# Sliding-window attention into a SwiGLU block: the opening's V loads moved behind a cast, and 11 dummy matmuls of 512 columns in place of 48 of 121

## The chip, the cores and the metric

The kernel runs on one core of one Trainium2 chip. The metric is the device time of one execution in microseconds (us). The three timed executions of the kernel before took 328.53, 329.00 and 329.53 us, a median of 329.0.

The core has five engines with a queue of instructions each: TensorE (PE; the profile lists its weight loads apart, as PEld), VectorE (DVE), ScalarE (ACT), GpSimd (POOL) and SyncE (SP). Transfers between main memory and the on-chip memory run on 16 DMA engines. Those that GpSimd issues run in one software queue, q0 in the profile.

## The reference

```python
# attention: 8 batches, 8 heads, 576 tokens, 64 per head; window of 64 tokens, causal
scores = np.matmul(q, k.transpose(0, 1, 3, 2)) / np.sqrt(64)
rel = pos[:, None] - pos[None, :]
scores = np.where((rel >= 0) & (rel < 64), scores, -1e9)
attn = softmax(scores)
attn_out = np.matmul(attn, v)                       # 8 x 8 x 576 x 64
# the block behind it, on 4608 tokens of 512
x = attn_out.transpose(0, 2, 1, 3).reshape(4608, 512)
g = x @ w_gate                                      # 512 -> 1536
out = (g * sigmoid(g) * (x @ w_val)) @ w_out        # 1536 -> 512
```

## The kernel before

The 4608 tokens are cut into 36 tiles of 128 tokens for the attention and into 9 chunks of 512 tokens (four tiles) for the block behind it. All matmuls are in bf16.

For a tile, `S` computes the scores of all heads into two PSUM banks (lines 468 and 472), ScalarE takes the exponential into `pt` (line 480), `AVs` multiplies by V, which carries a column of ones for the sum (line 592), and `AVn` divides on VectorE: a reciprocal (line 608) and a product (line 611) into `xb`. `X` transposes `xb` on TensorE (line 723), and a copy puts it into `xT`. For a chunk, `F` multiplies `xT` by columns of Wg and of Wv (line 787), ScalarE and VectorE form the gated product `hT`, and `O` multiplies it by Wo (line 818) and stores the result.

The first four tiles have an order of their own, written out by hand in `build`. A score needs keys from the tile and from the half tile before it, so the V rows that stand across a tile's border are copied into shifted tiles `vs`: `shift(n, r, engine)` copies half `r` of V tile `n` (line 295, called from line 579). Tile 1 reads `vs` that `shift(0, 1)` and `shift(1, 0)` fill, tile 2 that of `shift(1, 1)` and `shift(2, 0)`, tile 3 that of `shift(2, 1)` and `shift(3, 0)`.

The opening in `build` runs as follows. `loads` issues the first keys from SP and ACT (line 734), and then, on GpSimd, the first queries, the second keys and the second queries (line 375), the making of the identity and of the masks (lines 317 and 326), the loads of V tiles 0 to 3 (line 366), those of the first columns of Wg and Wv (line 381), and four shifts. VectorE finishes the masks meanwhile (lines 330 to 335). `warm` has TensorE run 48 matmuls of 121 columns on zeros (line 762). `first_T` casts the first keys to bf16 on VectorE (line 295, tile `ost`) and transposes them on TensorE (line 746); `T2` does the like with queries and keys of 256 tokens (line 415). `Sbias` puts the mask into a PSUM bank by a matmul (line 448). Then come the scores of tiles 0 and 1, further transposes, `AVs` of tile 0, the scores of tile 2, `AVs` of tile 1, the scores of tile 3, `X` of tiles 0 and 1, one dummy matmul, `AVs` of tiles 2 and 3, and `F` on the first 256 tokens.

After the opening, a list of steps in the text `EARLY` and a regular loop set the order on the engines, and the lists `LOADS` and `SHIPS` set the order of GpSimd's loads and of SP's transposing transfers. Every operation of an engine runs in the order in which it was added; a small planner works out the semaphore waits from what each operation reads and writes. `self.hold`, given to a load as `after`, makes it wait for a named operation as well.

Of the kernel before, what the change touches and what calls it, by code (L numbers as in the profile page):

```python
# [166 lines left out]
class _Kernel:  # L167
# [234 lines left out]
    def T2(self, st, x, engs):  # L402
        g = self.g
        src = (self.ks2 if x == "k" else self.qs2)[st % 2]
        dst = self.kT if x == "k" else self.qT
        z0 = (2 * st) % self.NZ
        for cc in range(2):
            bank, bk = self.bank("a")
            tb = bank[:, 0:256].bitcast(BF).rearrange("p (c j t) -> p c j t", c=2, j=2)

            def pe(e, cc=cc, tb=tb):
                for c in range(2):
                    for j in range(2):
                        for p in range(2):
                            r = e.transpose(tb[64 * p:64 * p + 64, c, j, :], src[:, 4 * cc + 2 * c + p, j, :], self.ident[:, :])  # L415
                return r

            g.op("pe", pe, reads=["ident", ("s2", x, st % 2, 0), ("s2", x, st % 2, 1)], writes=[bk])
            d = dst[:, 2 * cc:2 * cc + 2, 128 * z0:128 * z0 + 256].rearrange("p c (t j) -> p c t j", j=2)
            a = tb.rearrange("p c j t -> p c t j")  # L420
            self.copy(engs[cc], d, a, [bk], [(x + "T", z, cc) for z in (z0, z0 + 1)])
            self.drop([(bank, bk)])
# [282 lines left out]
    def X(self, n, eng="sp", kind="f", half=False):  # L705
        if n >= NCH:
            return
        g = self.g
        ix, it, u = n % 4, (n // 4) % self.NX, n % 4
        xb = self.xb[ix]  # L710
        xo = self.xT[it][:, :, 128 * u:128 * u + 128]
        xk = [("xb", ix, 0), ("xb", ix, 1)]
        if eng == "sp":
            g.op("sp", lambda e: e.dma_start_transpose(xo, xb[:, :]), reads=xk, writes=[("xT", it, u)], dma=True)
            return
        bank, bk = self.bank(kind)
        tb = bank[:, 0:256].bitcast(BF).rearrange("p (c t) -> p c t", c=4)

        def pe(e):
            for c in range(4):  # L720
                for p in range(2 if half else 1):
                    w = 64 if half else 128
                    r = e.transpose(tb[w * p:w * p + w, c, :], xb[:, 128 * c + w * p:128 * c + w * p + w], self.ident[:, :])  # L723
            return r

        g.op("pe", pe, reads=["ident"] + xk, writes=[bk])
        self.copy(eng, xo, tb, [bk], [("xT", it, u)])
        self.drop([(bank, bk)])
# [38 lines left out]
    def F(self, c, fs, lo=0, hi=512):  # L767
        g = self.g
        nf, n = len(fs), hi - lo
        w = nf * n  # L770
        xT = self.xT[c % self.NX]
        xk = [("xT", c % self.NX, u) for u in range(lo // 128, hi // 128)]
        ih = c % self.NH
        i = self.n_s % self.NS
        self.n_s += 1
        sig, uu = self.sig[i], self.uu[i]
        out = self.hT[ih][:, fs[0]:fs[0] + nf, lo:hi]
        v3 = lambda a: a[:, 0:w].rearrange("p (f t) -> p f t", f=nf)
        bs = []
        for W, wk in ((self.Wg, "Wg"), (self.Wv, "Wv")):  # L780
            bank, bk = self.bank("f")
            bs.append((bank, bk))

            def pe(e, W=W, bank=bank):
                for a, f in enumerate(fs):
                    for kk in range(NK):
                        r = e.matmul(bank[:, a * n:a * n + n], W[:, kk, f * 128:f * 128 + 128], xT[:, kk, lo:hi],  # L787
                                     start=(kk == 0), stop=(kk == NK - 1))
                return r

            g.op("pe", pe, reads=xk + [(wk, f) for f in fs], writes=[bk], cost=w * 0.0017)
            if wk == "Wg":
                g.op("act", lambda e, G=bank: e.activation(sig[:, 0:w], G[:, 0:w], ACTF.Tanh, scale=0.5), reads=[bk], writes=[("sig", i)])  # L793
        (G, gk), (V, vk) = bs
        g.op("dve", lambda e: e.scalar_tensor_tensor(uu[:, 0:w], sig[:, 0:w], 1.0, G[:, 0:w], ALU.add, ALU.mult),  # L795
             reads=[("sig", i), gk], writes=[("uu", i)])
        g.op("dve", lambda e: e.scalar_tensor_tensor(out, v3(uu), 0.5, v3(V), ALU.mult, ALU.mult),  # L797
             reads=[("uu", i), vk], writes=[("hT", ih, f) for f in fs])
        self.drop(bs)
# [61 lines left out]
    def loads(self):  # L861
        self.first_loads()
        self.load2(0, "q")
        self.load2(1, "k")
        self.load2(1, "q")
        self.init()
        self.init_ident()
        self.init_mask()
        self.init_nmask()
        for n in range(4):  # L870
            self.load(n, "v")
        self.W(0, 2)
        self.load_w("g", 2, 4)
        self.shift(0, 1, "pool")
        self.shift(1, 1, "pool")
        self.load_w("v", 2, 4)
        self.shift(2, 1, "pool")
        self.shift(3, 0, "pool")
        self.W(4, 6)
        self.W(6, 8)  # L880

# [178 lines left out]
    def build(self):  # L1060
        F, S, AV, X, T2, O = self.F, self.S, self.AV, self.X, self.T2, self.O
        self.loads()
        self.banks("a", [4, 5, 6, 7, 0, 1, 2, 3, 4, 5, 0, 1, 2, 3, 4, 5, 6, 7, 0, 1, 2, 3, 4, 5, 6, 7, 6, 7])
        self.warm(48, n=121)
        self.first_T(("dve", "act"))
        s0 = self.Sa(0)
        T2(0, "q", ("act", "dve"))
        self.Sbias(s0)
        self.warm(2)
        self.Sb(s0)  # L1070
        s1 = self.Sa(1, True)
        self.Sb(s1)
        T2(1, "k", ("dve", "act"))
        T2(1, "q", ("dve", "act"))
        self.start()
        s2, s3 = self.Sa(2), self.Sa(3)
        a0, a1, a2, a3 = self.AVa(0), self.AVa(1), self.AVa(2), self.AVa(3)
        self.AVs(a0)
        self.shift(1, 0, "dve")
        self.AVn(a0)  # L1080
        self.shift(2, 0, "dve")
        self.Sbias(s2)
        self.Sb(s2)
        self.AVs(a1)
        self.AVn(a1)
        self.Sbias(s3)
        self.Sb(s3)
        X(0, "dve", "a")
        X(1, "dve", "a")
        self.warm(1, j=2)  # L1090
        self.AVs(a2)
        self.AVn(a2)
        self.AVs(a3)
        self.AVn(a3)
        F(0, (0, 1), 0, 256)
        X(2, "act", "a")
        X(3, "act", "a")
        F(0, (2, 3), 0, 256)
        F(0, (0, 1), 256, 512)
        for n in range(4):  # L1100
            self.did |= {w % n for w in ("s%d", "a%d", "x%d", "Tk%d", "Tq%d")}
        self.main("F0.2-3b")
        self.free = set(range(8))
        self.g.now = dict.fromkeys(self.g.now, max(self.g.now.values()))
        for t in self.program():
            self.pump()
            first = len(self.g.ops)
            self.main(t)
            self.at[t] = next((o for o in self.g.ops[first:] if o.eng == "pe"), None)
        self.pump()  # L1110
        assert not any(self.queues)
        self.g.emit()
# [42 lines left out]
```

## Time and profile before

| what | value |
|---|---|
| median of three executions | 329.0 us |
| the profiled execution, its own time | 329.18 us |
| its span | 327.4 us |
| TensorE busy | 316.7 us, 97% of the span |
| VectorE, ScalarE, GpSimd busy | 203.3, 137.0, 107.6 us |
| granted TensorE clock | 1.00 |
| read from and written to main memory | 37.75 and 9.44 MB |

The profile is of one execution. Its span is 1.8 us shorter than the time of the same execution; what lies around the span isn't in the trace. Durations below are from this execution. In a timeline, the columns are the start and the duration in us, the engine, the line of the kernel, the operation with its output and inputs, the number of instructions merged, and in brackets how long the engine was idle before and what ended that; "issue" there is time in which the engine waited for nothing that the profile shows. In the table by stages, the number in brackets behind an engine's busy time is the count of its instructions.

### The profile page before, as it was taken

The page shows a single profiled execution, that of the slowest core. Times are in us where ns is not written, and L with a number is a line of the kernel's source. Part 1 is how long each engine was busy: PE and PEld are TensorE (multiplying, and loading weights), DVE is VectorE, ACT ScalarE, POOL GpSimd, SP SyncE. Part 2 cuts the span into 40 slices and gives each one's busy share as a digit, 9 for nine tenths or more (in the row PEclk, how much of TensorE's full clock was granted, in tenths as well). Part 3 has the DMA queues.
Part 4 walks back from the last instruction along what each step waited for, and adds up shares of the span by engine and source line. Part 5 has one row for each costly group of instructions (what it writes and reads, how often), then busy time and mean ns, then how long its engine had stood idle before and what let it go on. Part 6 is the DMA issues. An engine that isn't in the chain of part 4 may idle for free.

```text
span 327.4 us, 8016 instructions
## 1 busy us (share of the span) xinstructions
PE 316.7 (97%) x3413; PEld 168.1 (51%) x3451; DVE 203.3 (62%) x352; ACT 137.0 (42%) x246; POOL 107.6 (33%) x138
## 2 busy tenths in 40 slices
PE   7899999999999999999999999999999999999997
PEld 6584576666455445444545454545454544444443
DVE  4677975676567935775757666665656566555520
ACT  2645865555234445242525252525252432332222
POOL 8899969645300000507060607060602000000000
DMA  9999999999999762949899999999997211100012
GB/s 139 178 186 183 187 195 157 160 181 161 148 156 160 127 147 66 101 107 120 127 130 113 135 139 108 137 122 132 120 138 87 55 45 49 49 32 33 34 58 103
DMA packets 157348, 39.33 MB, mean 120 GB/s; under 512 B 144384, under 2 KB 152832, under 8 KB 157312
## 3 DMA queue, kind: packets, MB, share of 16 engines
q0 software_dynamic: 109008, 18.62, 73.8%
q1 hardware_dynamic: 42848, 10.69, 22.8%
q10 hardware_dynamic: 5456, 9.51, 9.3%
q8 instruction: 27, 0.44, 0.6%
q14 instruction: 9, 0.07, 0.1%
HBM read 37.75 MB, written 9.44 MB: 144 GB/s over the span
## 4 chain that ended last, share of the span: by engine, by line
PE 93%; issue 2%; ACT 2%; POOL 1%; DVE 1%; POOLq 0%
PE ps L787 56%; PE ps L818 28%; PE ps L641 3%; PE ps L505 1%; PE ps L468 1%; PE ps L415 1%; PE ps L723 1%; PE ps L843 1%; ACT pt L480 1%; PE ps L472 1%; PE ps L592 1%; POOL qs L375 1%; ACT kT L293 0%; ACT qT L293 0%; PE ps L509 0%
## 5 line engine op out<-in xcount | busy, mean ns | idle before, releaser
L787 PE MATMUL ps<-xT,Wv 128*128 128x512 bf16 (+1 forms) x470 | 110.6, 357 | 1.1 <-issue 0.6
L787 PE MATMUL ps<-xT,Wg 128*128 128x512 bf16 (+1 forms) x461 | 107.1, 357 | 2.7 <-issue 2.5
L795 DVE SCALAR_TENSOR_TENSOR uu<-sig,ps 128x512 bf16<-128x512 bf16 x108 | 73.8, 683 | 57.2 <-ACT sig L793 57.2
L793 ACT ACTIVATE sig<-ps 128x512 bf16<-128x512 f32 x108 | 65.1, 603 | 74.1 <-PE ps L787 74.0
L818 PE MATMUL ps<-Wo,hT 128*128 128x512 bf16 x413 | 95.2, 379 | 0.5 <-issue 0.2
L797 DVE SCALAR_TENSOR_TENSOR hT<-uu,ps 128x512 bf16<-128x512 bf16 x108 | 74.1, 686 | 3.7
L787 PEld LDWEIGHTS ps<-xT,Wv 128*128 128x128 bf16 x480 | 47.0, 98 | 46.4
L787 PEld LDWEIGHTS ps<-xT,Wg 128*128 128x128 bf16 x480 | 45.0, 98 | 43.1 <-issue 0.8
L818 PEld LDWEIGHTS ps<-Wo,hT 128*128 128x128 bf16 x420 | 40.9, 98 | 49.1
L366 POOL DMA_DIRECT2D kn<-in_k_dram x29 | 25.2, 874 | 114.7 <-PE ps L818 69.0
L825 ACT ACTIVATE ost<-ps 128x512 f32<-128x512 f32 x35 | 20.9, 597 | 92.2 <-PE ps L818 92.2
L366 POOL DMA_DIRECT2D va<-in_v_dram x40 | 35.0, 893 | 17.1 <-PE ps L818 10.9
L366 POOL DMA_DIRECT2D qn<-in_q_dram x29 | 25.3, 874 | 8.3 <-DMA Wo<-in_moe_w_out_dram 2.9
L668 DVE RECIPROCAL rp<-ps 128x14 f32<-128x14 f32 (+1 forms) x28 | 5.7, 202 | 33.5 <-PE ps L641 33.5
L480 ACT ACTIVATE pt<-ps 128x512 bf16<-128x512 f32 x36 | 18.9, 599 | 6.6 <-PE ps L472 5.7
L517 ACT ACTIVATE pt<-ps 128x512 bf16<-128x512 f32 x36 | 18.6, 603 | 3.7 <-PE ps L509 3.7
L670 DVE TENSOR_TENSOR xb<-ps,rp 128x896 bf16<-128x896 f32 (+1 forms) x28 | 19.4, 692 | 1.0
L641 PEld LDWEIGHTS ps<-va,pt 64*64 64x64 bf16 x888 | 10.8, 107 | 6.1 <-issue 5.5
L641 PE MATMUL ps<-va,pt 64*64 64x65 bf16 x888 | 13.4, 194 | 0.1
L526 DVE TENSOR_TENSOR pt<-pt,kmask 128x1024 bf16<-128x1024 bf16 x18 | 12.3, 683 | 0.0
L526 DVE TENSOR_TENSOR pt<-pt,mask 128x1024 bf16<-128x1024 bf16 x14 | 9.6, 686 | 2.0 <-ACT pt L480 2.0
L472 PE MATMUL ps<-qT,kT 64*64 64x64 bf16 x288 | 7.6, 194 | 1.0 <-issue 1.0
(65 smaller groups left out, 145.1 us busy)
## 6 DMA issues: line engine op xcount, KB each, us to landing
out_dram<-ost ACTq DMA_DIRECT2D x35, 256.0 KB, 3.1
va<-in_v_dram POOLq DMA_DIRECT2D x32, 128.0 KB, 6.1
kn<-in_k_dram POOLq DMA_DIRECT2D x23, 128.0 KB, 5.4
qn<-in_q_dram POOLq DMA_DIRECT2D x23, 128.0 KB, 5.5
Wg<-in_moe_w_gate_dram POOLq DMA_DIRECT2D x6, 256.0 KB, 7.3
Wv<-in_moe_w_val_dram POOLq DMA_DIRECT2D x6, 256.0 KB, 7.3
Wo<-in_moe_w_out_dram POOLq DMA_DIRECT2D x2, 768.0 KB, 15.4
qs<-in_q_dram POOLq DMA_DIRECT2D x3, 256.0 KB, 6.8
```

The costliest lines, as they stand in the source:

```text
L366: self.g.op("pool", lambda e, d=d, a=a: e.dma_start(d, a), writes=ks, dma=True, after=self.hold)
L480: g.op("act", lambda e, po=po, p=p: e.activation(po, sv[p], ACTF.Exp, scale=SCALE), reads=[bx[p][1]], writes=[pk[p]])
L517: g.op("act", lambda e, po=po, p=p: e.activation(po, sv[p], ACTF.Exp, scale=SCALE), reads=[bx[p][1]], writes=[pk[p]])
L526: self.g.op("dve", lambda e: e.tensor_tensor(pt, pt, m, ALU.mult), reads=pk + [key], writes=pk)
L641: z = e.matmul(self.psa[64 * c:64 * c + 64, o:o + 65], pt[p][rows, h, 64 * a:64 * a + 64], va[m][rows, h, 0:65], start=first, stop=phase = ...
L670: g.op("dve", lambda e, d=d, num=num, rb=rb: e.tensor_tensor(d, num, rb, ALU.mult), reads=bk + [("rp", k)], writes=xk, cost=(1.0, 0.25)[k])
L787: r = e.matmul(bank[:, a * n:a * n + n], W[:, kk, f * 128:f * 128 + 128], xT[:, kk, lo:hi], start=(kk == 0), stop=(kk == NK - 1))
L793: g.op("act", lambda e, G=bank: e.activation(sig[:, 0:w], G[:, 0:w], ACTF.Tanh, scale=0.5), reads=[bk], writes=[("sig", i)])
L795: g.op("dve", lambda e: e.scalar_tensor_tensor(uu[:, 0:w], sig[:, 0:w], 1.0, G[:, 0:w], ALU.add, ALU.mult), reads=[("sig", i), gk], writes ...
L797: g.op("dve", lambda e: e.scalar_tensor_tensor(out, v3(uu), 0.5, v3(V), ALU.mult, ALU.mult), reads=[("uu", i), vk], writes=[("hT", ih, f) ...
L818: r = e.matmul(OB[:, :], hT[:, f, 128 * u:128 * u + 128], self.Wo[:, f, :], start=(f == 0), stop=(f == NF - 1), skip_group_check=mid is no ...
L825: g.op("act", lambda e: e.activation(ost[:, :], OB[:, :], ACTF.Copy), reads=[ok], writes=[("ost", io)])
```

## The change

Three things are changed, all in the opening.

The loads of V tiles 0 to 3, and all that follows them on GpSimd in the opening, move from `loads` into a new function `next_loads`, which is called after `first_T`. On GpSimd they still stand behind the masks; but the first V load now waits for VectorE's cast of the first keys (the first VectorE operation that `first_T` adds), and since GpSimd works in order, all behind it do.

The dummy matmuls at the start are 11 of 512 columns, where they were 48 of 121.

`shift(0, 1)` is done by VectorE, ahead of `shift(1, 0)`, and no longer by GpSimd. On GpSimd `shift(1, 1)` now stands ahead of the second load of Wg, and the second load of Wv behind `shift(3, 0)`.

```diff
         self.init_ident()
         self.init_mask()
         self.init_nmask()
+
+    def next_loads(self, after):
+        self.hold = after
         for n in range(4):
             self.load(n, "v")
+            self.hold = None
         self.W(0, 2)
+        self.shift(1, 1, "pool")
         self.load_w("g", 2, 4)
-        self.shift(0, 1, "pool")
-        self.shift(1, 1, "pool")
-        self.load_w("v", 2, 4)
         self.shift(2, 1, "pool")
         self.shift(3, 0, "pool")
+        self.load_w("v", 2, 4)
         self.W(4, 6)
         self.W(6, 8)
 
@@ build @@
-        self.warm(48, n=121)
+        self.warm(11)
+        first = len(self.g.ops)
         self.first_T(("dve", "act"))
+        self.next_loads(next(o for o in self.g.ops[first:] if o.eng == "dve"))
         s0 = self.Sa(0)
         T2(0, "q", ("act", "dve"))
         self.Sbias(s0)
...
         a0, a1, a2, a3 = self.AVa(0), self.AVa(1), self.AVa(2), self.AVa(3)
         self.AVs(a0)
+        self.shift(0, 1, "dve")
         self.shift(1, 0, "dve")
         self.AVn(a0)
         self.shift(2, 0, "dve")
```

## The prediction

> **What bounds the kernel now.** First the page: TensorE is busy for 97% of the span and carries 93% of the chain that ended last. So what counts is when its dense stream starts, and where it stops. Second, its own waits: beyond the first 7 us there are two holes worth the name, 1.0 us at line 472 and 0.6 us at line 787, both ended by "issue", which is no other engine.
>
> ```profile
> span 327.4 us, 8016 instructions
> PE 93%; issue 2%; ACT 2%; POOL 1%; DVE 1%; POOLq 0%
> q8 instruction: 27, 0.44, 0.6%
> PE ps L787 <- issue: 3.1, 17, 0.6
> PE ps L472 <- issue: 1.0, 1, 1.0
> ```
>
> Third, the chain in the opening and the timeline around 83 us, which place the holes: 14.18 to 15.21 us, inside the scores of tile 3, and 0.55 us before 83.58, inside one product of four matmuls. Nothing in the program separates the matmuls there.
>
> ```profile
> 14.03 0.15 PE ps L468
> 14.18 1.03 issue
> 15.21 0.22 PE ps L472 x2
> ...
> 83.58 0.38 PE L787 MATMUL ps<-xT,Wv 128*128 128x512 bf16 x1 [0.55 <-issue]
> ```
>
> Fourth, TensorE's instruction counts by stage.
>
> ```profile
> 0.00:9.28 9.28, 6.94 (x92) 5.98 (x97) 4.63 (x18) 2.57 (x4) 7.86 (x15) 1.00 1.12 143
> 9.28:14.50 5.22, 4.55 (x145) 2.82 (x135) 3.60 (x8) 4.13 (x8) 4.60 (x7) 1.00 2.06 172
> 14.50:16.30 1.80, 0.96 (x29) 0.80 (x29) 0.73 (x2) 0.64 (x2) 1.38 (x3) 1.00 1.45 196
> 16.30:83.50 67.20, 65.59 (x970) 43.34 (x980) 48.06 (x87) 38.40 (x71) 50.52 (x64) 1.00 1.72 174
> ```
>
> Between the holes lie 29 + 980 = 1009 weight loads, each with a matmul: 2018 instructions, and some 30 separate waits make 2048, or 8 x 256. The instruction queue q8 moved 27 packets, 0.44 MB: 16 KB each, or 256 instructions of 64 bytes, and 27 x 256 = 6912 is about TensorE's whole program (2 x 3451). I read the holes as TensorE at the end of its loaded code. The code packets next to them began at 12.82 and 81.30 us and took 0.95 us; TensorE went on 1.44 and 1.34 us after their ends. The DMA engines were at their fullest when the first was asked for.
>
> Fifth, the opening by engine: POOL and DVE rows, one launch of V each time, then the copies.
>
> ```profile
> 5.38 0.91 POOL L366 DMA_DIRECT2D va<-in_v_dram  x1
> 5.38 2.04 POOL L366 DMA_DIRECT2D va<-in_v_dram  x2
> 5.33 0.22 DVE L330 TENSOR_SCALAR mask<-mask 128x192 bf16<-128x192 bf16 x1 [2.62 <-POOL mask L326]
> 5.86 0.49 DVE L335 TENSOR_SCALAR nmask<-mask 128x384 bf16<-128x384 bf16 x1
> 6.27 0.67 DVE L295 CAST ost<-hT 128x1024 bf16<-128x1024 f32 x1
> 12.04 0.72 DVE L295 COPY vs<-va 64x512 bf16<-64x512 bf16 x1
> 14.92 0.61 POOL L295 COPY vs<-va 64x512 bf16<-64x512 bf16 x1 [1.00 <-DMA va<-in_v_dram]
> 20.25 1.04 PE L787 MATMUL ps<-xT,Wv 128*128 128x256 bf16 x8
> ```
>
> The launches of V overlap the mask's last step and the cast, and the second lasted 1.13 us where the others last about 0.9.
>
> **The change part by part.**
>
> *Dummies.* 48 of 121 columns ran from 1.29 to 6.01 us: 101 ns apart up to 5.5 us, 53 ns after (the rate had doubled). 11 of 512 at the same rates: 427 ns each, ten by 5.6 us, the last soon after. Both end about 1 us before the transposes at 7.00: 0 us. But 37 matmuls and 37 loads fewer move every edge of the code 74 instructions later in the program. The first hole stood behind load 222; it now stands behind load 259 of the old count, in the middle of AVs of tile 2 (the opening has 251 loads by 16.30). The edge before it, where the next block is asked for, moves from load 97 (9.28 us) to load 134 (10.52 us, in the second keys' transposes). From 9.28 to the release took 5.93 us; so the block is there at about 10.52 + 5.93 = 16.45 us. This hole isn't removed; it meets the other chain, next.
>
> *Copy moved to VectorE.* One more copy, 0.65 us from start to start as at 12.04, lies on VectorE ahead of both divisions. In order: copies from 12.04 and 12.69, reciprocal 13.34, product 13.56, copy 14.16, reciprocal 14.65, product from 14.88 to 15.57 (before: to 14.92). X of tile 1 follows at 15.62; before, the hole held it until 15.74. From there 0.58 us to AVs of tile 2 and 0.86 us more to the first F, as in the trace: F at 17.06, against 17.18. With the block arriving at 16.45, where TensorE wants it at 16.32, F is at 17.19. The removed GpSimd copy (0.6 us) lay beside transfers: 0.
>
> *V loads behind the cast.* GpSimd idles from 5.3 us to the cast's end at 6.94, and launches V 1.56 us later. The first V packets moved at 8.5 us, when the queue was through with queries and keys, which landed last at 10.03. When the queue is empty (148.05 us) a launch's first packet comes 2.1 us after its start and the data after 4.5, here 9.0 and 11.4 against 10.89 before; AVs of tile 0 waits for it at 11.24. Bounds for the transfer's delay: 0, covered by the queue, and 0.5 us. I take 0.2, being nearer the covered row, and the scores of tile 2 behind AVs of tile 0 wait for ScalarE until 12.68 anyway, so 0 on the path.
> The price of what overlapped the launches is not shown apart. The mask's last step takes 0.49 us for 384 columns, the earlier one 0.22 for 192, which scales to 0.45; if instead it waited for the first launch to end (6.29, and its own end is 6.35), up to 0.33 is to be won. Bounds 0 and 0.33; I take 0.2, between a row that scales almost and two that fit a wait. It goes through: transposes, score and ScalarE's chain up to 12.7 follow the cast, and the edges move with them.
> The Trainium skill ("SBUF — State Buffer", Who interferes with whom) says that a VectorE copy, cast or scalar operation in its fast two-port mode and GpSimd block each other whole, and that launches from GpSimd suffer by it. The 1.13 us launch agrees; by this rule the gain is the upper bound, and the sum 0.13 us lower.
>
> *Order of weights.* The second Wv piece is launched behind the copy that waits for V tile 3 (14.92 before). V tile 3 landed late, spread over 2.4 us with the code packet among it; launched at 9.8, I put it at 14.3 us, the copy's end at 14.9 and the Wv launch there (before: 12.56). The piece landed at 19.75, in a queue that hands over 256 KB every 1.35 us; a launch at 15.48 landed 5.62 later, behind that queue. So it comes between 19.75 and 15.5 + 5.6 = 21.1, nearer the first, since the queue has work until then: 19.9. F wants it at 20.25 less the gain. Cover of about 0.15 us remains: 0.
>
> *The hole at 83.58.* Its edge moves 74 instructions on to 91.56 us, in a stage of plain products: 7.1 us for the last block's 137 loads there become 15 us. Gone: -0.55. TensorE has no other hole until the end, and the transposed tiles of the scores land at least 2.1 us ahead of use, so the gain goes through. At the new edges in the crowded stretch (to 110 us), my count finds at least 8.6 us for a block that needs up to 7.5, where TensorE's queue asks some 40 instructions ahead, as the later blocks show (packets 4 us ahead of an edge).
>
> *Sum:* dummies and copy 0, overlap -0.2, weights 0, hole -0.55: -0.75 us. The profiled execution took 329.18, 0.18 over the median; 329.18 - 0.75 = 328.4, and against the median 328.3.
>
> The Trainium skill ("Runtime: NRT & Kernel Launch", Instruction fetch mechanics) says that code comes in blocks of 16 KiB, that TensorE holds 128 KiB and that a block's edge is mostly hidden. The block's size agrees; the two holes 2048 instructions apart don't look hidden. By it the sum would be -0.2, which is the third rival.
>
> **The rivals.**
>
> *More is won.* The block for the opening comes 0.3 us sooner, since its packet now falls into weights rather than V's small packets (blocks later on waited 2 to 5 us), and the overlap gives 0.33: -0.12 - 0.33 - 0.55 = -1.0, down to 327.8. Against: the longer VectorE chain allows no more, and Wv's landing stops it.
>
> *Slower: a new hole at 96.9 us.* The edge there follows that at 91.56 by only 5.4 us, because scores and V products spend 131 loads in 5.5 us. If the block is asked for only when TensorE is at the edge, 6.4 to 7.5 us (what the blocks near by took) leave a hole of 1.0 to 2.1: +0.3 to +1.35, taken at 329.8. It decides once less than 1 us of lead is left. For: the DMA engines are full there. Against: packets that came ahead of their edge.
>
> *Nothing but the opening's trifle.* The holes aren't code, or stay in other places: -0.2, 328.8.
>
> *Opening held up.* The block takes 7.3 us, as near 80 us, or Wv comes at 21.1: +1.1 in the opening, so +0.4 in all: 329.4; with both, 330.
>
> **How the numbers follow.** Forecast 0.42, more won 0.27, new hole 0.13, trifle 0.06, held up 0.12. About 0.3%, or 1 us, is what a measurement tells from no change. Faster by that: most of "more won" and a fifth of the forecast, 0.33; slower: half the new hole, half of "held up", and some for what I haven't seen, 0.2; same 0.47. The likeliest case alone spans 327.9 to 328.8. The range leaves out the far tails: 327.4 to 329.9.
>
> **What would show it.** Right: no hole at line 472 near 14 us, a short or none in AVs of tile 2 near 16.4, none at 83; first F between 16.8 and 17.2; the cast ahead of 6.27. Wrong: F later than 17.5, Wv's products waiting near 20, or an "issue" hole of 1 us behind the attention at 97.

## The result, and the profile after

The changed kernel is slower: 329.97 us, the median of 21 executions (328.69 to 333.05), against 328.76 for the kernel before (328.23 to 329.95, also 21). The ratio is 1.0039, with a 95% interval of 1.0022 to 1.0056. That is +1.2 us; the forecast was -0.7.

The profiled execution of the changed kernel took 328.69 us, the lowest of its 21, so its trace shows less of the loss than the median has. I profiled the same kernel again (329.86 us, span 328.1) and read the loss there. The kernel before was profiled twice more as well (328.57 and 329.1 us).

The page of the profile after:

```profile
span 326.9 us, 7941 instructions
PE 90%; DMA 3%; POOL 2%; issue 2%; DVE 1%; ACT 1%; POOLq 0%
q8 instruction: 27, 0.44, 0.5%
```

TensorE's share of the chain that ended last is 90% where it was 93%, and transfers, which had no share worth a figure, have 3%. TensorE's waits in that trace, then the same view of the second trace of the changed kernel (us of idle time, times, longest):

```profile
PE ps L787 <- issue: 2.5, 16, 0.2
PE ps L787 <- DMA Wv<-in_moe_w_val_dram: 1.0, 2, 0.7
```

```profile
PE ps L787 <- DMA Wv<-in_moe_w_val_dram: 1.6, 1, 1.6
PE ps L723 <- DVE xb L611: 0.9, 1, 0.9
```

The longest "issue" hole is now 0.2 us: those at line 472 and at 83 us are gone. In their place TensorE waits for Wv (0.7 of the 1.0 us of the first trace and all of the second's 1.6 for its second piece), and in the second trace also for VectorE's division. The chain of the second trace says what Wv came so late for (start and duration in us):

```profile
6.04 0.70 DVE ost L295
6.73 0.29 issue
7.02 1.77 POOL va L366 x2
8.79 5.46 DMA va<-in_v_dram
14.26 0.05 issue
14.31 0.73 POOL vs L295
...
15.65 5.80 DMA Wv<-in_moe_w_val_dram
21.45 0.04 issue
21.49 2.58 PE ps L787 x22
```

It is one serial chain: the cast, the held launches of V, a V tile that lands at 14.26, GpSimd's two copies, and only behind them the launch of Wv, which lands at 21.45. TensorE's timeline shows the cost, and GpSimd's when Wv was launched; first the second trace of the kernel before, then the second of the changed one.

```profile
12.74 0.75 POOL L381 DMA_DIRECT2D Wv<-in_moe_w_val_dram  x1
16.35 1.05 PE L787 MATMUL ps<-xT,Wg 128*128 128x256 bf16 x8
19.43 1.04 PE L787 MATMUL ps<-xT,Wv 128*128 128x256 bf16 x8
82.76 0.38 PE L787 MATMUL ps<-xT,Wv 128*128 128x512 bf16 x1 [0.54 <-issue]
```

```profile
15.65 0.74 POOL L381 DMA_DIRECT2D Wv<-in_moe_w_val_dram  x1
21.49 1.05 PE L787 MATMUL ps<-xT,Wv 128*128 128x256 bf16 x8 [1.61 <-DMA Wv<-in_moe_w_val_dram]
```

A good measure for the whole is when `F` goes on after its first four groups of eight products (the first weight load of the fifth group): 20.2 us in the second and third trace of the kernel before (21.02 in the first, with its hole of 1 us), 21.18 and 22.27 in the two of the changed one. From there to the end of the span are 306.4, 306.6 and 307.1 us in the three traces of before (the third has another hole, of 0.4 us at line 641) and 305.8 after (both). So against the later two traces the opening loses 1.0 to 2.1 us, and the hole at 83 us gives back about 0.7; the second trace nets +1.3, which is its difference in span from the second trace of before (328.1 - 326.8).

### The profile page after: what moved, and what is told of

Read it like the earlier page. It is cut to its first block, busy times and chain, and to the rows that moved or that the text cites. A ratio compares the mean times of both kernels' runs of the same rounds, so it can differ in the third digit from the quotient of the medians.

```text
span 326.9 us, 7941 instructions
## 1 busy us (share of the span) xinstructions
PE 317.0 (97%) x3377; PEld 164.7 (50%) x3414; DVE 203.1 (62%) x353; ACT 137.0 (42%) x246; POOL 106.9 (33%) x137
## 4 chain that ended last, share of the span: by engine, by line
PE 90%; DMA 3%; POOL 2%; issue 2%; DVE 1%; ACT 1%; POOLq 0%
PE ps L787 55%; PE ps L818 28%; PE ps L641 3%; DMA Wv<-in_moe_w_val_dram 2%; DMA va<-in_v_dram 1%; PE ps L505 1%; PE ps L843 1%; POOL va L366 1%; PE ps L468 1%; PE ps L415 1%; POOL qs L375 1%; PE ps L723 1%; PE ps L472 0%; PE ps L509 0%; ACT kT L293 0%
## 5 line engine op out<-in xcount | busy, mean ns | idle before, releaser
L517 ACT ACTIVATE pt<-ps 128x512 bf16<-128x512 f32 x36 | 18.6, 603 | 3.7 <-PE ps L509 3.7
L641 PE MATMUL ps<-va,pt 64*64 64x65 bf16 x888 | 13.5, 194 | 0.1
## 6 DMA issues: line engine op xcount, KB each, us to landing
Wo<-in_moe_w_out_dram POOLq DMA_DIRECT2D x2, 768.0 KB, 16.5
```

The lines of the kernel that those rows point to most:

```text
L517: g.op("act", lambda e, po=po, p=p: e.activation(po, sv[p], ACTF.Exp, scale=SCALE), reads=[bx[p][1]], writes=[pk[p]])
L641: z = e.matmul(self.psa[64 * c:64 * c + 64, o:o + 65], pt[p][rows, h, 64 * a:64 * a + 64], va[m][rows, h, 0:65], start=first, stop=phase = ...
```

## The experiments

Three parts can each be put in or left out: the dummies, the wait for the cast ("the hold"), and the order (the second Wv piece behind `shift(3, 0)`, with `shift(0, 1)` on VectorE). My theory after the comparison was that the hold makes everything in the queue late and that the new order then puts Wv behind the latest V tile. The rivals were that the order alone does it, that the dummies and TensorE's clock do, and that the trace showed an accident. Differences below are from the kernel before in the same group of runs: 328.63, 328.58, 328.67 and 328.71 us in the four groups. Diffs are against the changed kernel.

### The changed kernel again

No edit.

> The changed kernel once more, for a second trace of it. Theory A (clock): in the first trace of the changed kernel the dummies run 427 ns apart to the last, and the granted clock is full only from 6.8 us, just ahead of the first transposes; in other executions it rises later, and the opening runs at half rate for a while. Then the executions spread over 2 us or more, the median is 329.7 to 330.3, and a trace with a long time shows transposes about 107 ns apart after 7 us. Theory B (a serial chain): the cast, the V launches, V tile 3's landing, GpSimd's copy, the second Wv launch and its landing now stand in a row; the spread is that of the landing. A trace with a long time then shows more than the 0.74 us of waiting for Wv near 20 us, at the usual rate of TensorE. Theory C (code): a long trace shows a hole ended by issue.

Measured: 330.21 us (329.25 to 330.56, 5 executions), ratio 1.0041 (1.0029 to 1.0053). The loss is no accident; its trace is the one read above. TensorE runs the transposes behind the dummies at the same rate as in the first trace (eight in 0.62 us, from 6.78), so the rate is not what this trace loses by.

### The dummies alone

The kernel before with one line of the change:

```diff
-        self.warm(48, n=121)
+        self.warm(11)
```

> The kernel before with 11 dummies of 512 columns for 48 of 121 and nothing else. A: slower than before by 0.8 to 1.5 us in the median, with a spread of 2 us or more. B: the loads stand as before, so no loss; the hole at 83.6 us goes (-0.55) and that at 14 us comes into play later: 328.0 to 328.5, narrow. C: a hole elsewhere, 329 to 330.

Measured: 328.13 us (327.63 to 330.4, 12), ratio 0.9991 (0.9976 to 1.0007); the profiled execution took 327.79. The interval takes in no change, so the times alone don't show a gain; the trace does. From the fifth group of `F` (20.35) to the end are 305.7 us, as in the changed kernel: the gain at 83 us belongs to the dummies. A hole in AVs of tile 2 stands where the prediction had put it, 0.53 us before 15.98:

```profile
15.25 0.20 PE L592 MATMUL ps<-vs,pt 128*64 128x65 bf16 x1
15.98 0.22 PE L592 MATMUL ps<-va,pt 128*64 128x65 bf16 x1 [0.53 <-issue]
```

So the dummies are not what loses the time.

### The loads without the dummies

The changed kernel with the old dummies:

```diff
-        self.warm(11)
+        self.warm(48, n=121)
```

> The changed kernel with the 48 dummies of 121 columns of before. A: no loss; the cast comes 0.2 us sooner, the code's edges stand as before with their two holes of 1.0 and 0.55 us: 328.3 to 329.0, narrow. B: as slow and as spread as the changed kernel, 329.7 to 330.3 or more, since the chain of launches is the same. C: holes as before, 329.

Measured: 330.52 us (329.78 to 331.48, 6), ratio 1.0057 (1.0044 to 1.007). TensorE's waits:

```profile
PE ps L787 <- DMA Wv<-in_moe_w_val_dram: 1.2, 1, 1.2
PE ps L592 <- DVE vs L295: 1.1, 1, 1.1
```

The loss is in the loads: +1.9 us, and with the 11 dummies it is +1.2 to +1.6. Neither of the two holes of before is in the list of waits, though the code's edges are back where they were. At the place of the one near 83 us, two groups start 1.15 us apart, where their neighbours are 0.86 apart:

```profile
82.88 1.03 PE L787 MATMUL ps<-xT,Wg 128*128 128x512 bf16 x4
83.74 1.03 PE L787 MATMUL ps<-xT,Wv 128*128 128x512 bf16 x4
84.89 1.04 PE L787 MATMUL ps<-xT,Wg 128*128 128x512 bf16 x4
```

That is a loss of 0.29 us, where the same measure gives 0.70 in the second trace of before. So the place of an edge does not settle what it costs.

### 13 dummies

```diff
-        self.warm(11)
+        self.warm(13)
```

> The changed kernel with 13 dummies of 512 columns for 11: two matmuls more (0.85 us at the slow rate, 0.43 at the full one) close the idle stretch of 0.6 us ahead of the first transposes; the code's edges move by 4 instructions. A: the clock has risen by the time of the transposes in nearly all executions: median 328.3 to 329.0, spread under 1.5 us. B: as the changed kernel, 329.7 to 330.3. C: as the changed kernel.

Measured: 329.85 us (329.39 to 330.31, 5), ratio 1.0034 (1.0022 to 1.0046). In the second trace of the changed kernel TensorE is idle for 1.55 us between the dummies and the transposes, here for 0.28, and the transposes begin at 6.78 in both. That does not mend it; Wv is waited for as before (1.2 us in two waits). The idle time behind the dummies is not the cause of this loss.

### Wv ahead of the late copies

```diff
         self.load_w("g", 2, 4)
+        self.load_w("v", 2, 4)
         self.shift(2, 1, "pool")
         self.shift(3, 0, "pool")
-        self.load_w("v", 2, 4)
```

> The changed kernel with the second Wv piece launched right behind the second Wg piece, ahead of the two GpSimd copies that wait for V tiles 2 and 3. Theory B1 (order): what costs is that the Wv launch stands behind the copy of V tile 3; here it is launched by 13.7 us instead of 15.1 to 15.8, lands by 20.1, and F waits for it 0.4 us at most: 328.0 to 328.6, so 0 to 0.7 us under the kernel before. Theory B2 (wait for the cast): what costs is that the V loads start 1.6 us later and push all weights back in the queue; the order then gives little: 329.3 to 330.

Measured: 329.04 us (328.37 to 329.68, 12), ratio 1.0009 (0.9997 to 1.0021). 0.75 to 1.1 us of the loss is recovered, so the order counts; the median lies between the two theories' ranges, so neither holds alone. But the wait for Wv hardly left because the piece came early: launched at 14.16, 1.5 us sooner than in the second trace, it still landed 6.6 us later, at 20.7. What TensorE waits for now is the division that stands behind VectorE's copy of V tile 2 (TensorE's waits, then VectorE's timeline):

```profile
PE ps L723 <- DVE xb L611: 1.6, 1, 1.6
```

```profile
15.18 0.29 DVE L295 COPY vs<-va 64x512 bf16<-64x512 bf16 x1 [1.33 <-DMA va<-in_v_dram]
```

### No hold

```diff
-        self.hold = after
         for n in range(4):
             self.load(n, "v")
-            self.hold = None
```

> The changed kernel without the wait for the cast: V is launched at 5.4 us as in the kernel before, the rest of the new order stands. B1: V tile 3 still lands at 13.7 to 14.9 us, the copy ends at 14.4 to 15.5 and Wv is launched there; F waits 0.3 to 1.2 us for it near 20 us: 328.7 to 329.8. B2: the weights come as before: 327.8 to 328.4.

Measured: 328.42 us (327.92 to 330.73, 12), ratio 1.0006 (0.9987 to 1.0024); profiled 327.98. One wait less brings back 1.4 to 1.7 us of the changed kernel's +1.2 to +1.6, with the new order kept. The launch of Wv at 14.56 lands in 4.7 us here, at 19.3. That is earlier than the 20.7 of the experiment above, where it was launched earlier, behind the same transfers. The queue itself is late under the hold: by 1.4 us between these two. What all transfers moved between 7 and 15 us, in the second trace of the changed kernel and in this one:

```profile
DMA packets 6327, 1.23 MB, mean 154 GB/s; under 512 B 5753, under 2 KB 6326, under 8 KB 6326
```

```profile
DMA packets 6646, 1.39 MB, mean 173 GB/s; under 512 B 5770, under 2 KB 6645, under 8 KB 6645
```

0.16 MB at 0.173 MB per us is 0.9 us. Over the traces: 1.36 to 1.40 MB without the hold (three of before, five other kernels), 1.15 to 1.23 with it (seven). The table by stages places the shortfall; the last column is GB/s, first the second trace of before, then that of the changed kernel:

```profile
9.50:10.50 1.00, 1.00 (x33) 0.54 (x32) 0.00 (x0) 0.93 (x2) 1.00 (x2) 1.00 2.40 155
10.50:11.50 1.00, 1.00 (x45) 1.00 (x45) 0.67 (x2) 1.00 (x3) 0.96 (x3) 1.00 2.44 155
11.50:12.50 1.00, 0.80 (x17) 0.25 (x11) 0.97 (x5) 1.00 (x3) 1.00 (x2) 1.00 2.38 172
12.50:13.50 1.00, 0.83 (x41) 0.75 (x42) 1.00 (x2) 0.46 (x2) 1.00 (x3) 1.00 1.62 184
```

```profile
9.50:10.50 1.00, 1.00 (x38) 0.68 (x38) 0.00 (x0) 1.00 (x3) 1.00 (x2) 1.00 2.20 144
10.50:11.50 1.00, 1.00 (x44) 0.94 (x38) 0.89 (x2) 1.00 (x3) 1.00 (x3) 1.00 2.24 142
11.50:12.50 1.00, 0.66 (x11) 0.16 (x10) 0.95 (x3) 0.90 (x2) 0.96 (x2) 1.00 2.08 145
12.50:13.50 1.00, 0.99 (x41) 0.73 (x42) 0.97 (x3) 0.56 (x2) 0.90 (x2) 1.00 1.59 120
```

These four stretches moved 0.55 MB where they moved 0.67. My reading is that the queue has too little to work on, since the launches from 7.02 on come one by one, 0.87 us apart, where before they had a lead of 1.6 us. That is not the whole of it: the column before the last is the time that the packets took, as a share of the 16 DMA engines' time. It is only about a tenth lower in the first three stretches, and hardly lower in the fourth, which moved a third less. What was not moved then, every later piece waits for: the three pieces of weights behind V (launch plus time to landing) land at 15.8, 17.2 and 18.6 us in both traces of the changed kernel, against 15.1 to 15.2, 16.5 and 17.8 to 17.9 in the second and third of before, 0.7 us late each.

### The hold with the order of before

```diff
         self.W(0, 2)
-        self.shift(1, 1, "pool")
         self.load_w("g", 2, 4)
+        self.shift(0, 1, "pool")
+        self.shift(1, 1, "pool")
+        self.load_w("v", 2, 4)
         self.shift(2, 1, "pool")
         self.shift(3, 0, "pool")
-        self.load_w("v", 2, 4)
...
-        self.shift(0, 1, "dve")
```

> The changed kernel with the wait for the cast and the 11 dummies, but with the order of the kernel before behind it: both shifts of half 1 on GpSimd behind the second Wg launch, Wv ahead of the shifts that need V tiles 2 and 3. B1: Wv is launched near 14.1 us and lands by 20.2: 328.1 to 328.9. B2: 329.3 to 330.

Measured: 329.13 us (328.45 to 329.96, 12), ratio 1.0014 (1.0 to 1.0028). With the runs above this fills a table of two by two, all with 11 dummies, as differences from the kernel before:

| | order of before | new order |
|---|---|---|
| no hold | -0.5 | -0.2 |
| hold | +0.55 | +1.2 to +1.6 |

The hold alone costs 1.05 us (in the trace, 0.7 us of it is AVs of tile 1 waiting for GpSimd's copy), the order alone 0.3, both together 1.7 to 2.1. Each of these medians is uncertain by about 0.5 us, as the intervals of the ratios show. So the cost of the hold and of both together are clear, but neither the 0.3 nor that both together cost more than their sum (by 0.35 to 0.75) is shown. Such a surplus would fit, since the order puts Wv behind exactly the transfers that the hold delays.

### No hold, and Wv ahead

The two edits of "no hold" and of "Wv ahead" together.

> The 11 dummies and the copy on VectorE alone: no wait for the cast, and the second Wv piece right behind the second Wg piece. Both theories: weights early, VectorE's chain free of GpSimd's copies; 327.5 to 328.2, faster than the kernel before by 0.5 to 1.1 us and at least as fast as the dummies alone.

Measured: 328.17 us (327.74 to 329.71, 12), ratio 0.9988 (0.9972 to 1.0005). Without the hold the place of Wv is worth 0.25 us, which is within the noise; with it, 0.75 to 1.1. The profiled execution was the slowest of the 12, for a reason of its own, told at the end.

### Wv ahead, and VectorE's copy of V tile 2 later

"Wv ahead", and besides:

```diff
         self.AVn(a0)
-        self.shift(2, 0, "dve")
...
+        self.shift(2, 0, "dve")
```

where the new place is behind `X` of tiles 0 and 1.

> The changed kernel with Wv ahead as in wv_ahead, and VectorE's copy of V tile 2, shift(2, 0), moved behind tile 1's division and the copies of X. Theory B3: what the wait for the cast still costs there is that VectorE stands at this copy until V tile 2 has landed (1.33 us in that trace) with tile 1's division behind it. Then the copy waits where less is behind it: 328.2 to 328.7, and the hole ahead of X of tile 1 is under 0.4 us. Rival B4: the cost is in the weights, which land 0.5 to 1 us later in the queue: 328.9 to 329.2 as before this edit.

Measured: 329.4 us (328.51 to 329.82, 12), ratio 1.0021 (1.0012 to 1.0029): no gain; 0.3 above "Wv ahead", which the intervals do not tell from none. Both theories had put it lower. TensorE's waits:

```profile
PE ps L592 <- DVE vs L295: 1.2, 1, 1.2
PE ps L787 <- DMA Wv<-in_moe_w_val_dram: 0.8, 1, 0.8
```

The division no longer waits, but AVs of tile 2 does, for the same copy, and then `F` for Wv, which was launched at 13.76 and landed 7.1 us later. This reordering only changed which user meets the late transfers first.

### Only tiles 1 to 3 held

```diff
+        self.load(0, "v")
         self.hold = after
-        for n in range(4):
+        for n in range(1, 4):
```

> The changed kernel, but V tile 0 is launched at once, at 5.4 us, and only tiles 1 to 3 and what is behind them wait for the cast. Theory E (starved queue): what the wait costs is that the queue of transfers runs dry near 10 us, when queries and keys are through and V tiles come one by one from their launches; 1.39 MB moved from 7 to 15 us without the wait, 1.18 to 1.23 with it. One tile more in the queue (0.83 us of work) bridges it: at least 1.33 MB from 7 to 15 us, the second Wv piece lands by 19.9 us, and the median is 328.2 to 328.7. Rival B1 (the serial row from the cast over V tile 3 and its copy to the Wv launch): tile 3 is launched at about 8.8 us instead of 9.65, Wv still behind its copy, and most of the loss stays: 329.2 to 329.8.

Measured: 328.81 us (328.26 to 329.36, 11), ratio 1.0004 (0.9995 to 1.0013). One launch ahead of the wait recovers 1.1 to 1.5 us. Between 7 and 15 us 1.31 MB moved, between the two groups above and a little under what I had expected, and the median lies between the ranges of the two theories. The landings part the two costs better than the bytes do: the three pieces of weights behind V land at 15.2, 16.5 and 17.9 us, as early as without the hold (15.8, 16.5 and 17.9 in "no hold"). So with one tile in hand the queue is no longer late, although it moved less. What is left meets mainly the second Wv piece, which is launched behind the copies: it goes out 0.4 us later than in "no hold" but lands 1.7 us later, at 21.0 and not by 19.9 as theory E had it, and TensorE waits for it (the profiled execution, 329.25 us, is near the top of its range):

```profile
14.30 0.73 POOL L295 COPY vs<-va 64x512 bf16<-64x512 bf16 x1 [0.92 <-DMA va<-in_v_dram]
14.99 0.74 POOL L381 DMA_DIRECT2D Wv<-in_moe_w_val_dram  x1
21.08 0.39 PE L787 MATMUL ps<-xT,Wv 128*128 128x256 bf16 x2 [1.20 <-DMA Wv<-in_moe_w_val_dram]
```

### 13 dummies, no hold, Wv ahead

```diff
-        self.hold = after
-            self.hold = None
...
-        self.warm(11)
+        self.warm(13)
```

and Wv ahead.

> No wait for the cast, Wv ahead, the copy on VectorE, and 13 dummies of 512 columns. Theory D (late clock): single executions above 329.3 us come from a full clock that is granted only at about 10.7 us, because the dummies end at 6.0 and TensorE idles until 7.0; 13 dummies leave no such gap. Median 327.9 to 328.3 and none above 328.9. Rival: the tail is the transfers' own; then one or two in twelve stand above 329.3 again, as with 11 dummies.

Measured: 328.09 us (327.76 to 328.86, 11), ratio 0.9983 (0.9974 to 0.9991). This beats both kernels, by 0.6 us against before. Its profiled execution was its highest, 328.86, and shows a hole that was not in the traces above:

```profile
35.91 0.38 PE L787 MATMUL ps<-xT,Wg 128*128 128x512 bf16 x1 [0.78 <-issue]
```

### 48 dummies, no hold, Wv ahead

The same with the dummies of before.

> No wait for the cast, Wv ahead, the copy on VectorE, and the 48 dummies of 121 columns. Against the same with 11 (328.17) and 13 (328.09) dummies it shows what the edges of the code are worth where the loads are in time. Theory F (edges): the hole before instruction 2500, near 83 us, is back with 0.5 to 0.6 us, and the median is 328.5 to 328.9. Rival: the dummies are worth nothing but the clock's rise; 328.0 to 328.3 with no such hole.

Measured: 328.68 us (327.87 to 329.42, 11), ratio 0.9999 (0.9989 to 1.0009): the whole gain of the last kernel is the dummies'. The hole near 83 us is back:

```profile
82.90 0.39 PE L787 MATMUL ps<-xT,Wg 128*128 128x512 bf16 x1 [0.38 <-issue]
```

## Why the prediction was wrong

*The step that failed* is "V loads behind the cast", in its last line: a delay of the transfers of 0.2 us within bounds of 0 and 0.5, "being nearer the covered row", and 0 on the path. I worked out when the first V packet would move and compared only that. The step that counts is the queue's supply after it: the first V tile does come in time, but with four launches 0.87 us apart and no lead the queue moves less until 13.5 us. The weights behind V land 0.7 us later than in the later two traces of before, and the hold alone costs 1.05 us of time. Both bounds were rows for one transfer; none asked how much the queue holds in reserve.

*Order of weights*, 0, failed too, and not only as a consequence. It had the chain right (the launch behind the copy that waits for V tile 3, forecast at 14.9) and priced it with a queue that "has work until then": landing at 19.9. The piece ahead of it landed at 18.6 in both traces; one piece of 1.35 us later is just that 19.9. But the launches came at 15.11 and 15.65 and the landings at 20.36 and 21.45: 0.4 and 1.5 us behind that turn, 5.2 and 5.8 us after the launch. With the hold kept, the launch ahead of the copies brings back 0.75 to 1.1 us. The upper end of this term, 21.1, stood in the rival "Opening held up" as a mishap of +0.4 in all, with 0.12; the second trace lies beyond it. It was the right rival, undersized.

*The hole at 83.58*, -0.55: right. It is absent in every trace with 11 or 13 dummies and there in every trace of before (0.54 to 0.60); with 48 dummies and changed loads it is 0.38 us in one trace and 0.12 in the other. The reading as code holds up too: the holes shown above, at 15.98, 35.91 and 82.90 us, stand at multiples of 256 instructions, within two, from the one before 82.76 in TensorE's program (counted in weight loads, each with its matmul, and separate waits). The rule of the Trainium skill ("Runtime: NRT & Kernel Launch", Instruction fetch mechanics) that an edge is mostly hidden does not hold for these: 0.4 to 0.8 us each are in the open, though at most edges no hole shows. The rival "new hole at 96.9" didn't come, nor did "nothing but the opening's trifle".

*Overlap*, -0.2: right in size.

```profile
5.86 0.26 DVE L335 TENSOR_SCALAR nmask<-mask 128x384 bf16<-128x384 bf16 x1
6.04 0.69 DVE L295 CAST ost<-hT 128x1024 bf16<-128x1024 f32 x1
```

The mask's last step takes 0.26 us without launches beside it, where it took 0.49, and the cast begins 0.23 earlier. That lies between the two values that were weighed, 0.2 and the 0.33 that the whole exclusion told of in the Trainium skill ("SBUF — State Buffer", Who interferes with whom) would give. The gain reached the first products of `F` in the lowest trace (15.99) and was then lost at the wait for Wv.

*Dummies*, 0 on the opening, and the *copy on VectorE*: right in effect. The copy was priced too high, at 0.65 us: the moved one took 0.29 us in both traces, as copies do that meet none of GpSimd's. The third copy, of V tile 2, shows the like:

```profile
14.28 0.28 DVE L295 COPY vs<-va 64x512 bf16<-64x512 bf16 x1 [0.59 <-DMA va<-in_v_dram]
```

Its bracket is another way in which a late V tile costs: VectorE works in order, and tile 1's division stands behind a copy that waits for V. (In the third trace of the kernel before, a copy waited 0.52 us for V as well.)

*The trace that I predicted from* misled: its hole of 1.03 us near 14 us is 0.18 us in both later traces of the kernel before, so the opening's edges were worth less than they seemed. And the cover of about 0.15 us for Wv came from it: there `F` wanted the piece at 20.25, in the later two traces at 19.43, so that even a landing at 19.9 would have been 0.5 us late. (One sum of the rivals does not come out either: -1.0 from the median is 328.0, not the 327.8 of "More is won".)

What stays open: why V's tiles land as unevenly as they do under the hold (V tile 2 anywhere from 13.0 to 15.2 us in the seven traces). A code packet begins between 11.6 and 13.1 us in these traces, among the V tiles. In the three traces with 11 dummies and no hold it begins at 13.7 or later, when V tile 3 has landed or is about to, and there the V tiles land an even 0.8 to 0.9 us apart. That would fit a packet that holds up the tile beside it, but no run moved the packet alone. Nor is it shown why the second Wv piece, launched behind the copies, takes 4.7 us to land in "no hold" and 6.0 with only tiles 1 to 3 held.

## What to carry to other kernels

Before you hold back a load, count what its queue still has to move, not only when the held load's first byte is wanted: here the queue was busy for a whole stage, and what it failed to move early made everything behind it late. Put a launch that others wait for ahead of work that waits for a transfer, since on an engine that works in order it inherits that wait. And profile the kernel before more than once: a hole of 1 us in one trace may be 0.2 us in the next.

## What the runs showed that I had not expected

The 11 dummies do not always bring TensorE to its full rate in time. In the profiled execution of "no hold, and Wv ahead" the transposes behind them ran at about half their rate, as did all matmuls until 10.7 us (the table by stages still gives a granted clock of 1.00 there, so this is read from the matmuls alone); its row first, then that of the changed kernel's first trace:

```profile
7.00 1.04 PE L746 MATMUL ps<-ident,ost 128*128 128x128 bf16 x8 [0.83 <-DVE ost L295]
```

```profile
6.78 0.62 PE L746 MATMUL ps<-ident,ost 128*128 128x128 bf16 x8 [0.61 <-DVE ost L295]
```

With the same dummies the rate doubled at times between 4.1 and 7.0 us in the other traces. The late one makes the opening 1.9 us longer, and its execution took 329.71 us against a median of 328.17. A late rise would fit the high tails of kernels with 11 dummies (330.4 and 330.73 among 12 each); with 13 dummies and no hold none of 11 lay above 328.86. That is a comparison of few executions, and what sets the moment of the rise isn't shown. The two slowest of the changed kernel's 21, 332.47 and 333.05 us, are the only ones of them with a granted clock under 0.999 (0.994 and 0.995); with 21 executions they don't move the median.
